# Contiguous groups of four from the ninth period on, in an attention kernel that shares its exponentials between two engines

## The chip, the cores and the metric

The kernel runs on one core of a Trainium2 chip. Its engines are TensorE (PE, matrix products), VectorE (DVE), ScalarE (ACT), GpSimd (POOL) and SyncE (SP, which issues transfers); they run side by side and meet at semaphores. The metric is the device time of one execution in microseconds (us), the median over several runs. Beside it there is one profiled execution, whose trace gives the duration of every instruction.

## The reference

Two attention blocks with the same input are mixed by a gate, position by position:

```python
x = A_x                                        # 1 x 2048 x 512, bf16
g = sigmoid((x * gate_w).sum(-1, keepdims=True))
a = _A_ref(x, A_wqkv, A_wo)                    # full attention, 32 heads of 16
b = _B_ref(x, B_wqkv, B_wo)                    # each position looks at 8 keys: itself and 2, 4 ... 14 back
return g * a + (1 - g) * b
```

Part A is a full softmax attention over 2048 x 2048 scores for each of 32 heads. Part B takes for every position a softmax over only eight keys, two positions apart.

## The kernel before, in words

**Part A.** The work is cut into 32 periods: four chunks of 512 queries times eight groups of four heads. A period has 64 blocks, one for each of 16 tiles of 128 keys and each of four heads; a block is 128 keys x 512 queries. The last period is done in two halves of 256 queries, so the program has 33 entries in its tables. For most blocks PE makes the scores in a PSUM tile `ring`, ACT takes their exponential into `pT` (three blocks in one instruction and two in the next, in turn), and PE multiplies `pT` with the values `vp_all` and adds up in one accumulator bank of the period. At the end of a period DVE transposes the accumulator out of PSUM (`accT`), takes a reciprocal (`rden`), POOL scales (`rden`, `ott`), and DVE transposes the result into `oat`, which the output projection reads.

**Blocks on DVE.** `n_dve` says how many blocks of each period go past ACT. They are taken from the last four key tiles and are worked on in groups (`d_set`): three blocks a group (`NGR`) in periods below `FLAT0`, four (`NGF`) from there on. For each block PE makes the scores in a spare PSUM bank, and DVE turns them into the bits of a bf16 power of two with one multiply-add to integers (`p1`, 512 elements, written to the group's buffer `dt`). When a group is full, three integer additions (`sh`, `NV` - 1 of them) make three shifted copies of the whole group in `pd_a`, and PE multiplies the four versions with differently weighted values (`vp_all`, `vd_all`); their sum approximates the exponential. In a group of three, a pass reads the 1536 elements as six rows of 256 and writes rows that lie 514 elements apart; in a group of four, a pass reads and writes one run of 2048 elements.

The group buffers `dt` lie in `dt_a` for early periods, then in `dt_a` and in `wkv` (the weights of the key and value projections, 4096 elements a partition, which are no longer needed by then). For groups of four they lie in `bw`, the weights of part B, free only when the last projection of part B is done.

**Part B.** Sixteen tiles of 128 positions. SP loads shifted keys and values (`ksh`, `vsh`), POOL forms products and sums (`prod`, `lg`, `av`, `obb`), DVE and ACT do the small softmax (`mx`, `ssum`, `rr`, and `lg`), POOL issues some additions as transfers (`av<-prod`, `av<-av`; the last two tiles add on POOL instead). PE transposes `obb`, DVE copies it to `obt`, and the output projection adds it to part A. `b_start` and `b_space` give the planned time of each tile.

**The order.** Nothing is ordered at run time. Every step is recorded with an engine, a due time and a cost; `list_schedule` plays them through by its own cost figures (`SB`, `PT`, `TT`, `GP` and others, where a part marked `True` occupies a port that DVE and POOL share in the plan) and the resulting order is written into the program. Each engine executes its list strictly in that order and waits where an operand is not there.

Of the kernel before, what the change touches and what calls it, by code (L numbers as in the profile page):

```python
# [12 lines left out]
BF16 = mybir.dt.bfloat16  # L13
# [3 lines left out]

CFG = dict(
    set_sizes=(3, 2),
    n_dve=(3, 3, 6, 6, 9, 9, 12, 12) + (12,) * 19 + (16,) * 4 + (8, 4),  # L20
    dve_tiles=4,
    b_start=36.0,
    b_space=(43.0,) * 16,
    chain=("pe", "dve", "act", "pool", "sp"),
)

# [1 line left out]
DH = 16  # L28
NG = 8
W = 8  # L30
DIL = 2
QW = 512
NEG = -1.0e9
FLAT0 = 27
BITS = 128.0
LN2 = 0.6931471805599453
SHIFT = 175.0
# [1 line left out]
NV = 4  # L39
NGR = 3  # L40
NGF = 4
NK1 = 2
# [7 lines left out]
NDE = 1  # L50
NDL = 3
# [57 lines left out]
PVU, PVN = 100.0, 4  # L109
GP = lambda kind, n: [(False, PRE), (True, NS[kind] * n)]  # L110
SB = lambda n: [(True, 0.065 + n / 3840.0)]
PT = lambda n: [(True, 0.1 + n / 3840.0)]
TT = lambda n: [(True, 0.075 + n / 960.0)]
PASS, SWITCH, KEEP, RIDE, ALONE = 0.22, 0.1, 1.2, 50.0, 3.0
WAIT, FREE, LATE, CLAMP = 0.15, 0.1, 10.0, -1.0
# [192 lines left out]
def kernel(  # L308
# [19 lines left out]
    DC = D // 128  # L328
# [6 lines left out]
    const = ctx.enter_context(tc.tile_pool(name="const", bufs=1))  # L335
# [90 lines left out]
    n_dve = cfg["n_dve"]  # L426
# [4 lines left out]
    for pi in range(NP):  # L431
        first_unit.append(nu)
        n = n_dve[pi]
        gr = group_of(pi)
# [16 lines left out]
    for pi, (own, groups) in enumerate(seq):  # L451
        n = sum(len(g) for g in groups)
# [22 lines left out]

    wkv = const.tile([128, DC, 2 * D], BF16, name="wkv")
    wq = const.tile([128, DC, D], BF16, name="wq")
    wq2 = const.tile([128, DC, 8, 2, DH], BF16, name="wq2")
    q_scr = tc.dram_tile([NG * NC // 2 * 16, DH * QW], BF16, name="q_scr")
    wk3 = const.tile([128, DC, NK1, 2, DH], BF16, name="wk3")  # L480
    a_w3 = A_wqkv.rearrange("(c p) n -> p c n", p=128)
    wkp = const.tile([128, DC, (NG - NK1) // 2, 4, 2, DH], BF16, name="wkp")
    gw = const.tile([128, DC], BF16, name="gw")
    bw = const.tile([128, DC, 3 * D], BF16, name="bw")
    bwo = const.tile([128, DC, D], BF16, name="bwo")
# [22 lines left out]
    wkv_l = wkv[:].rearrange("p c n -> p (c n)")  # L508
    dt_bufs = [dt_a[:, k_ * NGR * QW:(k_ + 1) * NGR * QW] for k_ in range(NDE)]
# [319 lines left out]
    for h0, h1, pn in ((4, 8, 1), (8, 16, 2), (16, 24, 4), (24, 32, 6)):  # L829
        TB = 512 // ((h1 - h0) * DH)  # L830
        for tb in range(0, NT, TB):
            late = tb + TB > NT - NTD
# [3 lines left out]
    qt_tiles, o_q, q_tok, last_q = {}, {}, {}, [None]  # L836
# [120 lines left out]
    a = None  # L957
    for sc in range(NC):
        a = op("pe", 0.9, zmm(sc), GT + sc, full=1, deps=[o_bw, a] + o_xt[sc], alloc=[tzp] if sc == 0 else [],
               use=[tzp] if sc else [], rel=20.0)  # L960
    a = op("act", 0.25, zsig, GT + 5, deps=[a], use=[tzp])
    o_g = op("dve", 0.8, zgate, GT + 6, deps=[a])
    a = op("pe", 1.2, zrows, GT + 8, full=1, deps=[o_g, o_init_p], alloc=[tzr])
    o_gr = op("dve", 0.12, zcopy, GT + 9, deps=[a], use=[tzr])


    o_kvd, o_obt, bw_users = [], [], []
    obt_tiles, obt_tok = {}, {}
    WP = WH // 2
    HB = D // 2  # L970
# [1 line left out]
    def b_tile(t):  # L972
# [27 lines left out]
        a = op("pe", WAVE(2), proj("pk", 1, 0), tb - 34 - KB, full=2, deps=[o_bw] + o_xt[cb], alloc=[tk, tkv], rel=rel)  # L1000
        a = op("pe", WAVE(2), proj("pk", 1, 2), tb - 33.5 - KB, full=2, deps=[a], use=[tk])
        ka = op("dve", 0.61, ke, tb - 33 - KB, deps=[a], use=[tk, tkv])
        tk = tok("misc", 2)
        a = op("pe", WAVE(2), proj("pv", 2, 0), tb - 32 - KB, full=2, deps=[o_bw] + o_xt[cb], alloc=[tk], rel=rel, after=[a])
        a = op("pe", WAVE(2), proj("pv", 2, 2), tb - 31.5 - KB, full=2, deps=[a], use=[tk])
# [4 lines left out]

        def qe():
            V.tensor_scalar(out=st["qb"][:], in0=st["pq"][:], scalar1=float(DH) ** -0.5, scalar2=None, op0=ALU.mult)
        bw_users.append(a)
        tk = tok("misc", 2)
        a = op("pe", WAVE(2), proj("pq", 0, 0), tb - 24 - QB, full=2, deps=[o_bw] + o_xt[cb], alloc=[tk, tqb], rel=rel)
        a = op("pe", WAVE(2), proj("pq", 0, 2), tb - 23.5 - QB, full=2, deps=[a], use=[tk])
        bw_users.append(a)
        qa = op("dve", 0.61, qe, tb - 23 - QB, deps=[a], use=[tk, tqb])

        def load(key, off, hf):  # L1020
# [154 lines left out]
        for g_ in range(len(halves)):  # L1175
# [5 lines left out]
        a = op("dve", 0.34, sm_pre, tb + SMD, deps=[l1], use=[tlg])  # L1181
        a = op("dve", 0.0, sm_sub, tb + SMD, deps=[a], use=[tlg], parts=TT(H * W)) if SM_V else op(
            "pool", 0.0, sm_sub, GFIRST, deps=[a], use=[tlg], parts=GP("ff", H * W))
# [126 lines left out]
                pv_run(pend[q_:min(n, q_ + 4)], tn)  # L1310
            del pend[:n]

    bw_l = bw[:].rearrange("p c n -> p (c n)")
    wkv_users = [o for o in ops if o.eng == "pe" and o.name.startswith(("kp", "vp"))]
    d_st, d_last, d_sh = {}, [None, None], []
    d_count, d_ends = [0, 0, 0, 0], []

    def d_set(pi, gi, t, j, qk_, tn):

        c_, i = periods[pi]  # L1320
        late = pi >= LATE0
        flat, gr = pi >= FLAT0, group_of(pi)
        key = (pi, gi)
        first = key not in d_st
        if first:
            slot = d_count[3] % NDL if flat else d_count[0] % NDL if late else d_count[2] % NDE
            d_count[3] += flat
            d_count[0] += late and not flat
            d_count[2] += not late
            d_st[key] = dict(dt=bw_l[:, slot * gr * QW:(slot + 1) * gr * QW] if flat else dt_bufs[slot],  # L1330
                             td=tok("dtf", NDL) if flat else tok("dtl", NDL) if late else tok("dt", NDE), js=[], ts=[], p1=[])
        g = d_st[key]
        n_ = len(g["js"])
        g["js"].append(j)
        g["ts"].append(t)

        st = {}
        tx = tok("misc", 2)

        def dq():  # L1340
            st["x"] = misc_ps([128, QW])
            for t_, cs in parts_of(pi, t):
                mm(st["x"][:, cs], kt_all[32 * j:32 * j + 32, i, t_ * 128:(t_ + 1) * 128], qt_tiles[pi][32 * j:32 * j + 32, q_cols(pi)],
                   True, True, tile_position=(32 * j, 0))

        def p1():
            V.tensor_scalar(out=g["dt"][:, n_ * QW:(n_ + 1) * QW].bitcast(U16), in0=st["x"][:], scalar1=float(DH) ** -0.5 * BITS / LN2,
                            scalar2=(127.0 + DEXP + SHIFT * float(DH) ** -0.5 / LN2) * BITS, op0=ALU.mult, op1=ALU.add)
        deps = [o_q[pi], o_k[i][tiles_of(pi, t)[0] // TPC]] + [o_vd[(4 * i + j, t_)] for t_ in tiles_of(pi, t)]
        if first and flat and d_count[3] <= NDL:  # L1350
            deps += bw_users
        elif first and late and d_count[0] <= NDL:
            deps += wkv_users + d_ends[-NV * NDE:]
        a = op("pe", 0.0, dq, tn - 3.0, mode="r", js=[j], deps=deps, alloc=[tx] + ([g["td"]] if first else []),
               use=[q_tok[pi]] + ([] if first else [g["td"]]), after=[qk_, d_last[1]], ride=True, name=f"dq{pi}")
        d_last[1] = a
        o = op("dve", 0.61, p1, tn + P1D, deps=[a], use=[tx, g["td"]], after=[d_last[0]], name=f"p1_{pi}")
        d_last[0] = o
        g["p1"].append(o)
        if len(g["js"]) < gr:  # L1360
            return
        vs = [o_vd[(4 * i + j_, t2)] for t_, j_ in zip(g["ts"], g["js"]) for t2 in tiles_of(pi, t_)]

        def sh(m, pb):
            def s():
                o_, i_ = pb.bitcast(U16)[:, :, 0:QW], g["dt"].bitcast(U16)
                if not flat:
                    i_ = _ap(i_, [list(i_.ap[0]), [QW // 2, 2 * NGR], [1, QW // 2]])
                else:
                    o_ = o_.rearrange("p q n -> p (q n)")  # L1370
                V.tensor_scalar(out=o_, in0=i_, scalar1=STEP * m, scalar2=None, op0=ALU.add)
            return s

        def pv(m, pb):
            def s():
                pv_mm(pi, [(t_, j_, pb[:, n1, 0:QW]) for n1, (t_, j_) in enumerate(zip(g["ts"], g["js"]))],
                      lambda t2: vd_all[:, m - 1, t2 - (NT - NTD)] if m else vp_all[:, t2])
            return s

        def dpv(m, pb, deps, use, dl):  # L1380
            b = op("pe", 0.0, pv(m, pb), dl, mode="c", js=g["js"], full=1, deps=deps + [o_t0[pi]] + vs,
                   use=[use, acc_tok[pi]], name=f"dpv{pi}")
            o_pv[pi].append(b)
            d_ends.append(b)
        dpv(0, g["dt"].rearrange("p (q n) -> p q n", q=gr), list(g["p1"]), g["td"], tn + 4.5)
        for m in range(1, NV):
            pb = pd_bufs[d_count[1] % NPD]
            if flat:
                k0 = d_count[1] % NPD * gr * QW
                pb = pd_a[:, k0:k0 + gr * QW].rearrange("p (q n) -> p q n", q=gr)  # L1390
            d_count[1] += 1
            tp = tok("pd", NPD)
            a = op("dve", 0.0, sh(m, pb), tn + 1.5 + SHD * (m - 1), deps=list(g["p1"]), alloc=[tp], use=[g["td"]],
                   lat=(0.065 + NGR * QW / 1920.0 if not flat else 0.1 + gr * QW / 3840.0) + SH_LAT, after=d_sh[-1:],
                   parts=[(False, 0.065 + NGR * QW / 1920.0)] if not flat else PT(gr * QW), name=f"sh{pi}")
            d_sh.append(a)
            dpv(m, pb, [a], tp, tn + 4.5 + SHD * m)
# [216 lines left out]
```

## Time and profile before

| | before |
|---|---|
| time, median of 3 runs | 800.21 us (799.62 to 801.82) |
| the profiled execution: time / span of its instructions | 803.18 / 800.3 us |
| busy PE / DVE / ACT / POOL, share of the span | 93% / 87% / 97% / 81% |
| exponentials on ACT, `pT<-ring` | 674 instructions, 766.5 us |
| integer passes `pd_a` in groups of three | 288 (138 from `dt_a`, 150 from `wkv`), mean 0.94 us |
| integer passes `pd_a` in groups of four, from `bw` | 57, mean 0.744 us |
| granted TensorE clock, mean | 0.998 |

The span runs from the first to the last instruction; the time of the execution has 2.9 us more. Busy shares are the union of an engine's instructions, and two that follow each other closely overlap by some hundredths of a microsecond in the records, so a mean duration is a little more than what one instruction costs in a row. The first group of four is worked on from 684 us on.

### The profile page before, as it was taken

The numbers are of one execution on the slowest core, as the hardware profiler recorded it, in microseconds if no ns is written. First come the engines' busy times: TensorE is split into PE (matmuls) and PEld (weight loads), VectorE is DVE, ScalarE is ACT, GpSimd is POOL, SyncE is SP. The second block draws the span as 40 slices with busy tenths as digits, with TensorE's granted clock in tenths as the row PEclk, the third lists the DMA queues.
The fourth block names the chain that finished last, engine by engine and source line by source line (L and its number), as shares of the span: only waits on it lengthen the run. The fifth ranks groups of instructions, "written<-read, shape, count | busy, mean of one in ns | idle before, by whom it ended". The sixth has DMA issues, their size and how long they took to land.

```text
span 800.3 us, 17773 instructions
## 1 busy us (share of the span) xinstructions
PE 741.5 (93%) x6817; PEld 241.9 (30%) x6876; DVE 692.6 (87%) x1100; ACT 774.5 (97%) x697; POOL 644.3 (81%) x1067
## 2 busy tenths in 40 slices
PE   8999989999999999999999999998999999999997
PEld 4333333233222222222222232232232232222233
DVE  5638787998887899999998899899898999988986
ACT  3999999999999999999999999999999999999996
POOL 4098989899999997899989899999989999991000
PEclk9999999999999999999999999999999999999999
DMA  8413071625344535336352626253625371100000
GB/s 265 115 46 106 21 177 47 156 64 128 98 113 118 131 83 143 81 97 142 73 146 77 162 74 165 66 117 112 144 65 109 107 169 35 47 8 20 2 2 28
DMA packets 58886, 77.21 MB, mean 96 GB/s; under 512 B 3744, under 2 KB 50848, under 8 KB 58800
## 3 DMA queue, kind: packets, MB, share of 16 engines
q1 hardware_dynamic: 52608, 53.91, 21.6%
q0 software_dynamic: 6048, 22.02, 14.8%
q8 instruction: 53, 0.87, 0.4%
q14 instruction: 33, 0.27, 0.1%
q10 hardware_dynamic: 144, 0.13, 0.0%
HBM read 43.78 MB, written 10.26 MB: 68 GB/s over the span
## 4 chain that ended last, share of the span: by engine, by line
ACT 50%; PE 23%; issue 22%; DVE 4%; DMA 1%; SPq 0%; ACTq 0%; DVEq 0%
ACT pT L370 49%; PE misc_ps L379 15%; PE ring L379 7%; DVE pd_a L370 1%; DMA xld<-in_A_x_dram 1%; DVE dt_a L370 1%; ACT lg L370 1%; DVE vd_all L370 1%; DVE wkv L370 0%; DVE kt_all L370 0%; PE pxt L647 0%; DVE vp_all L370 0%; DVE ssum L370 0%; DVE rr L370 0%; DVE osb L370 0%
## 5 line engine op out<-in xcount | busy, mean ns | idle before, releaser
L370 ACT ACTIVATE pT<-ring 128x1536 bf16<-128x1536 f32 (+1 forms) x674 | 766.5, 1327 | 10.5 <-PE ring L379 7.3
L379 PE MATMUL ring<-qt,kt_all 32*128 32x512 bf16 (+1 forms) x1736 | 265.5, 375 | 41.3 <-ACT pT L370 32.8
L379 PE MATMUL misc_ps<-pT,vp_all 128*17 128x512 bf16 (+3 forms) x1736 | 201.9, 377 | 0.3 <-DVE dt_a L370 0.2
L370 POOL TENSOR_TENSOR prod<-ksh,qb 128x256 f32<-128x256 bf16 x256 | 175.7, 757 | 30.0 <-DMA ksh<-kv_scr 27.2
L379 PEld LDWEIGHTS <-kt_all 32*128 32x128 bf16 x2112 | 92.2, 91 | 291.2 <-issue 281.6
L370 POOL TENSOR_TENSOR prod<-prod 128x256 f32<-128x256 f32 (+1 forms) x256 | 172.8, 690 | 5.9
L370 DVE TENSOR_SCALAR pd_a<-wkv 128x1536 uint16<-128x1536 uint16 x150 | 137.2, 940 | 1.0 <-PE misc_ps L379 0.6
L379 PE MATMUL misc_ps<-qt,kt_all 32*128 32x512 bf16 (+1 forms) x376 | 130.5, 374 | 3.8 <-DVE dt_a L370 2.2
L379 PE MATMUL misc_ps<-pd_a,vd_all 128*17 128x512 bf16 (+1 forms) x1128 | 131.1, 375 | 0.5 <-DVE pd_a L370 0.4
L379 PE MATMUL misc_ps<-z 128*32 128x512 bf16 x382 | 127.9, 388 | 1.6 <-DVE z L370 1.6
L370 DVE TENSOR_SCALAR pd_a<-dt_a 128x1536 uint16<-128x1536 uint16 x138 | 126.5, 939 | 0.6
L370 DVE TENSOR_SCALAR wkv<-misc_ps 128x512 uint16<-128x512 f32 x150 | 100.1, 681 | 18.5 <-PE misc_ps L379 17.6
L370 DVE TENSOR_SCALAR dt_a<-misc_ps 128x512 uint16<-128x512 f32 x138 | 92.1, 682 | 21.0 <-PE misc_ps L379 19.6
L370 POOL TENSOR_TENSOR prod<-vsh,lg 128x256 f32<-128x256 bf16 x128 | 84.1, 772 | 0.0
L379 PEld LDWEIGHTS <-vp_all 128*17 128x17 bf16 (+1 forms) x2112 | 55.9, 88 | 84.8 <-issue 71.9
L370 POOL TENSOR_TENSOR av<-vsh,lg 128x256 f32<-128x256 bf16 x128 | 80.0, 664 | 0.0
L370 DVE TENSOR_SCALAR bw<-misc_ps 128x512 uint16<-128x512 f32 x76 | 50.8, 684 | 10.8 <-PE misc_ps L379 10.2
L379 PE MATMUL misc_ps<-bw,xT 128*128 128x512 bf16 x163 | 50.6, 384 | 1.9 <-issue 1.4
L379 PEld LDWEIGHTS <-vd_all 128*17 128x17 bf16 x1128 | 34.9, 88 | 53.4 <-issue 46.6
L379 PEld LDWEIGHTS <-z 128*32 128x32 bf16 x382 | 32.9, 96 | 45.5 <-issue 26.5
L370 DVE TENSOR_SCALAR pd_a<-bw 128x2048 uint16<-128x2048 uint16 x57 | 41.2, 744 | 0.1
L370 POOL TENSOR_TENSOR rden<-rden,g_rw 128x16 f32<-128x16 f32 x30 | 9.3, 310 | 37.5 <-DVE rden L370 37.4
(100 smaller groups left out, 596.0 us busy)
## 6 DMA issues: line engine op xcount, KB each, us to landing
ksh<-kv_scr SPq DMA_DIRECT2D x32, 512.0 KB
vsh<-kv_scr SPq DMA_DIRECT2D x32, 512.0 KB
av<-prod POOLq DMA_DIRECT2D x28, 512.0 KB, 6.2
av<-av POOLq DMA_DIRECT2D x14, 512.0 KB, 5.0
kv_scr<-kvs SPq DMA_DIRECT2D x16, 256.0 KB
qt<-q_scr SPq DMA_DIRECT2D x30, 128.0 KB
out_dram<-osb SPq DMA_DIRECT2D x15, 128.0 KB
xld<-in_A_x_dram SPq DMA_DIRECT2D x3, 512.0 KB
```

The costliest lines, as they stand in the source:

```text
L370: return chain_on(key, f(*a, **k))
L379: return chain(nc.tensor.matmul(out, lhsT=lhsT, rhs=rhs, start=start, stop=stop, **kw))
```

## The change

Groups of four begin with period 8 instead of period 27. In periods 8 to 26, `n_dve` alternates between 12 and 16 where it was 12, so that 400 blocks go to DVE instead of 364. The spacing of the last twelve tiles of part B in the plan is 46 us instead of 43. In the plan, a contiguous pass costs 0.5 us off the shared port and 0.25 us on it, where it was 0.633 us on it. The buffers of groups of four are now two in `wkv` and one in a new tile `wx`, which holds what were the tiles `wq2` and `wkp` (weights for the projections of the early periods); the first three groups wait until these weights have been used. The instructions of POOL are the same 1073 as before.

```diff
 CFG = dict(
-    n_dve=(3, 3, 6, 6, 9, 9, 12, 12) + (12,) * 19 + (16,) * 4 + (8, 4),
+    n_dve=(3, 3, 6, 6, 9, 9, 12, 12) + (12, 16) * 9 + (12,) + (16,) * 4 + (8, 4),
-    b_space=(43.0,) * 16,
+    b_space=(43.0,) * 4 + (46.0,) * 12,
...
-FLAT0 = 27
+FLAT0 = 8
...
-PT = lambda n: [(True, 0.1 + n / 3840.0)]
+PT = lambda n: [(False, 0.5), (True, 0.25)]
...
-    wq2 = const.tile([128, DC, 8, 2, DH], BF16, name="wq2")
+    n_q2, n_kp = DC * 8 * 2 * DH, DC * (NG - NK1) // 2 * 8 * DH
+    wx = const.tile([128, n_q2 + n_kp], BF16, name="wx")
+    wq2 = wx[:, 0:n_q2].rearrange("p (c h e d) -> p c h e d", c=DC, h=8, e=2)
+    wkp = wx[:, n_q2:n_q2 + n_kp].rearrange("p (c i j e d) -> p c i j e d", c=DC, i=(NG - NK1) // 2, j=4, e=2)
...
-    bw_l = bw[:].rearrange("p c n -> p (c n)")
+    dt_flat = [wkv_l[:, 0:NGF * QW], wkv_l[:, NGF * QW:2 * NGF * QW], wx[:, 0:NGF * QW]]
...
-            d_st[key] = dict(dt=bw_l[:, slot * gr * QW:(slot + 1) * gr * QW] if flat else dt_bufs[slot],
+            d_st[key] = dict(dt=dt_flat[slot] if flat else dt_bufs[slot],
...
-        if first and flat and d_count[3] <= NDL:
-            deps += bw_users
-        elif first and late and d_count[0] <= NDL:
-            deps += wkv_users + d_ends[-NV * NDE:]
+        if first and late and d_count[3 if flat else 0] <= NDL:
+            deps += wkv_users + [o_q[1]] + d_ends[-NV * NDE:]
```

More of the change, by code (lines that the diff above doesn't have):

```diff
@@ L481 @@
     a_w3 = A_wqkv.rearrange("(c p) n -> p c n", p=128)
-    wkp = const.tile([128, DC, (NG - NK1) // 2, 4, 2, DH], BF16, name="wkp")
     gw = const.tile([128, DC], BF16, name="gw")
@@ L964 @@
     o_gr = op("dve", 0.12, zcopy, GT + 9, deps=[a], use=[tzr])
-    o_kvd, o_obt, bw_users = [], [], []
+    o_kvd, o_obt = [], []
     obt_tiles, obt_tok = {}, {}
@@ L1012, in qe @@
             V.tensor_scalar(out=st["qb"][:], in0=st["pq"][:], scalar1=float(DH) ** -0.5, scalar2=None, op0=ALU.mult)
-        bw_users.append(a)
         tk = tok("misc", 2)
@@ L1016, in b_tile @@
         a = op("pe", WAVE(2), proj("pq", 0, 2), tb - 23.5 - QB, full=2, deps=[a], use=[tk])
-        bw_users.append(a)
         qa = op("dve", 0.61, qe, tb - 23 - QB, deps=[a], use=[tk, tqb])
```

## The prediction

> **What bounds the kernel now.** First the page's busy shares, then its chain of waits, then the slices.
>
> ```profile
> PE 741.5 (93%) x6817; PEld 241.9 (30%) x6876; DVE 692.6 (87%) x1100; ACT 774.5 (97%) x697; POOL 644.3 (81%) x1067
> ACT  3999999999999999999999999999999999999996
> POOL 4098989899999997899989899999989999991000
> ACT 50%; PE 23%; issue 22%; DVE 4%; DMA 1%; SPq 0%; ACTq 0%; DVEq 0%
> ```
>
> ACT is the bound: 97% busy, and half of the chain. POOL is the second thing to see: it is full from slice 2 to slice 36 and then has nothing left. Its 81% is an average of "full" and "done". The last instruction of part B on POOL is an `obb` pair at 721.56 us, 1.41 us long, so POOL ends its tiles at 723.0, 77 us ahead of the end. That is all the slack it has.
>
> The groups by form give the prices on ACT and DVE; the same view cut to two stretches shows the contiguous pass beside a working POOL (684 to 722) and beside an idle one (722 to 801):
>
> ```profile
> L370 ACT ACTIVATE pT<-ring 128x1536 bf16<-128x1536 f32 x337 | 518.3, 1538 | 9.8 <-PE ring L379 7.3 <-PE misc_ps L379 1.9
> L370 ACT ACTIVATE pT<-ring 128x1024 bf16<-128x1024 f32 x336 | 375.5, 1117 | 0.7 <-PE misc_ps L379 0.3
> L370 DVE TENSOR_SCALAR pd_a<-wkv 128x1536 uint16<-128x1536 uint16 x150 | 137.2, 940 | 1.0 <-PE misc_ps L379 0.6
> ...
> L370 DVE TENSOR_SCALAR pd_a<-bw 128x2048 uint16<-128x2048 uint16 x16 | 14.3, 908 | 0.1
> ...
> L370 DVE TENSOR_SCALAR pd_a<-bw 128x2048 uint16<-128x2048 uint16 x41 | 27.0, 680 | 0.1
> ```
>
> The same instruction takes 0.68 us alone and 0.91 beside POOL. The timelines of the two engines around 700 us show the other half of it:
>
> ```profile
> 698.60 0.68 DVE L370 TENSOR_SCALAR pd_a<-bw 128x2048 uint16<-128x2048 uint16 x1
> 699.80 3.23 DVE L370 TENSOR_SCALAR pd_a<-bw 128x2048 uint16<-128x2048 uint16 x3
> 703.54 1.13 DVE L370 TENSOR_SCALAR pd_a<-bw 128x2048 uint16<-128x2048 uint16 x1
> ...
> 698.04 7.13 POOL L370 TENSOR_TENSOR av<-vsh,lg 128x256 f32<-128x256 bf16 x8
> 705.13 2.88 POOL L370 TENSOR_TENSOR prod<-vsh,lg 128x256 f32<-128x256 bf16 x4
> 712.28 2.44 POOL L370 TENSOR_TENSOR prod<-vsh,lg 128x256 f32<-128x256 bf16 x4
> 714.68 1.86 POOL L370 TENSOR_TENSOR av<-av,prod 128x256 f32<-128x256 f32 x2
> ```
>
> From 712.28 to 714.68 POOL makes four products with no pass beside them: 0.60 us each. From 698.04 to 705.13 it makes eight such, with five passes beside them, and needs 7.09 us instead of 4.80: **each contiguous pass costs POOL 0.46 us**. Over all of 684 to 722, POOL's groups exceed their undisturbed durations (the medians of 0.65 for the two products, 0.72 for f32 adds) by 8 x 0.28 + 11 x 0.11 + 12 x 0.08 + 8 x 0.24 = 6.3 us, and two small steps by 0.35 (`rden`, 0.57 instead of 0.22) and 0.2 (`rr`): 6.9 us for 16 passes, 0.43 each. I take 0.45. The passes of groups of three show no such thing: with some 160 of them in 300 to 640, `av<-vsh` keeps its mean of 0.65.
>
> **ACT.** 36 blocks less: 766.5 us for 1684 blocks is 0.455 a block, so **-16.4 us**. If ACT stays the bound, that is the gain in full.
>
> **DVE.** In the built program 228 passes of 1536 go (288 to 60) and 198 of 2048 come (57 to 255). A pass of three costs 0.88 in a row (1.80 us for two, 2.65 for three in the timeline): -200 us. The new passes take 0.60 in a row beside an idle POOL and 1.05 in the worst row (3.23 for three); taken at 0.908 less an overlap of 0.08, +164. 36 more `p1` at 0.60: +22. Sum -14 us, bounds -59 and +30. DVE was busy 422.9 us of the 459 between 225 and 684, so at the middle value it keeps pace, no better.
>
> **PE.** A group of four has its four heads in four column groups, so its products run side by side; in periods 8 to 26 there are 66 groups x 4 sets of products instead of 76 x 4. 36 more score products ride with the others. Filler products on zeros go from 380 to 334. Nothing here is near the end.
>
> **Buffers.** The first group of four now waits for `wkv` and `wx` to be free. The last products that read `wkv` are at 182 us and period 8 starts at about 225: no cost; if they came late, three groups would wait at most.
>
> **POOL.** It has the same instructions, and 255 - 16 = 239 more passes to suffer. At 0.45 all colliding cost 107.6 us; POOL was idle 35.7 of the 497 us from 225 to 722, so some 7% of the passes may fall into a gap: **+100 us**. What can be recovered are waits for DVE, since a late POOL finds these results ready:
>
> ```profile
> POOL av L370 <- DMA av<-prod: 7.8, 4, 3.1
> POOL av L370 <- POOL prod L370: 5.7, 19, 0.3
> POOL rden L370 <- DVE rden L370: 4.9, 9, 1.5
> POOL lg L370 <- DVE mx L370: 3.1, 5, 0.8
> POOL prod L370 <- DVE qb L370: 2.0, 1, 2.0
> POOL rr L370 <- DVE rr L370: 1.7, 3, 0.8
> ```
>
> The last four sum to 11.7; POOL's own chains and its transfers remain. So POOL ends at 723 + 100 - 12 = **811 us**. Bounds: with no gap found and nothing recovered 831; with 0.40 a pass, one pass in ten free and all 35.7 us of idle time gone, 773, where ACT would decide.
>
> One page of the Trainium skill speaks against this change. "SBUF — State Buffer", section "Who interferes with whom", says that a DVE operation in a two-port mode and GpSimd exclude each other for the whole instruction. By that rule the price would be the full record, 0.68 us, and POOL would end some 50 us later still; the 0.46 of the row decides, as the records of neighbouring instructions overlap. The same page ("SBUF: two separate sides") says that transfers issued by GpSimd starve too, as it cannot write their descriptors. No trace here shows it, because the last such issue is at 644 us, ahead of the first pass; by it no issue would be a gap, and the 7% would go, for some 7 us more.
>
> **The order decides that POOL's delay counts.** In DVE's built list the last `obt` copy, part B's last tile, stands third from the end behind all 255 passes; before, it stood behind 26 of 57 contiguous passes with two more periods to come. PE's last real work is the transpose of that `obb`, the projection of `obt`, and one product of `oat`. So the plan already puts the end of POOL right ahead of the end of the program, and it charges a pass 0.25 us on the shared port where the trace shows 0.45. And DVE runs its list in order: `mx` waits for POOL's `lg`, `oat` for POOL's `ott`. When POOL is late, DVE stands at these with the `p1` and evictions queued behind; then PE has no free bank and ACT no scores. ACT can't run ahead and simply finish early.
>
> **The tail** behind POOL's last `obb`: four transposes 0.4, `obt` 0.41, seven projections 1.7 (0.82 for three at 794.02), eviction 0.69, last product 0.38, and from the final add (796.79) to the span's end 3.5; with five handovers of some 0.2, 8 us. The span becomes 811 + 8 = 819. The profiled execution has 2.9 us around its span and lies 3.0 above the median, so the median is the span: **819 us**, 19 slower.
>
> **Rivals.**
> 1. *ACT keeps the bound (faster).* POOL's slack of 77 us swallows the locks and the end is 800.2 - 16.4 = **784 us**. For: ACT is the bound today, and POOL had slack. Against: POOL would have to end by 784 - 8 = 776, that is, 239 passes may cost (776 - 711)/239 = 0.27 us each. The trace has 0.43 to 0.46. It decides if four passes in ten miss POOL.
> 2. *DVE becomes the bound.* POOL pays less than the row says but DVE pays its full 0.91 waiting: 422.9 - 200 + 180 + 22 = 425 us of work, at the 92% that it reached 461 us long, where ACT needs 443: 784 + 18 = **802 us**. It decides above 0.82 a pass, just under what I took; against it, the wait of DVE and the delay of POOL come from the same collisions.
> 3. *The passes lose their fast form* in `wkv` and `wx`: 1.25 us each (4/3 of 0.94), DVE +63 and some **850 us**. Against: type, size and layout are those of the row from `bw`.
>
> **Chances.** POOL bound 0.74, ACT bound 0.16, DVE bound 0.08, slow form 0.02. POOL's own range is 800 to 838, from 0.40 a pass with half the idle time recovered to everything colliding. The whole range reaches into rival 1, to 790, leaving out about 0.13 below and 0.05 above. A difference under 0.3% (797.8 to 802.6) can't be told from none. Faster: rival 1 and a little of the main case, 0.18. Same: half of rival 2 and the low end of the main case, 0.06. Slower: 0.76.
>
> **What would show it.** POOL's digits at 9 up to the last slices and its last `obb` within 10 us of the end; `av<-vsh` and `prod` groups longer by 0.2 to 0.3 in the mean; `pd_a` from `wkv` and `wx` at 0.9; DVE waiting for POOL in `mx` and `oat`; ACT with 40 us or more of idle time. It is wrong if POOL is done by 775, or if its groups keep their means beside the passes.

## The result and the profile after

The changed kernel takes **851.2 us** (848.5 to 854.0) against 800.7 for the kernel before in the same runs: a ratio of 1.063, 95% interval 1.059 to 1.067. The forecast had the right sign and the wrong size: 819, with 838 as the upper end. The profiled execution has 851.43 us and a span of 849.4.

The page's busy shares, slices and chain:

```profile
PE 755.9 (89%) x6885; PEld 232.9 (27%) x6939; DVE 736.2 (87%) x1106; ACT 765.1 (90%) x682; POOL 731.1 (86%) x1067
ACT  3999999999999798998999969989798989979993
POOL 4198999998999886899899979989798988969996
DVE 33%; PE 28%; ACT 24%; issue 14%; DMA 1%; SPq 0%; ACTq 0%; DVEq 0%
```

POOL now works to the end; its last `obb` ends at 841.9 us. But no engine is full. ACT has lost its 97%, POOL has 86%, and the chain, half of it ACT before, now runs through DVE for a third. This is what engines that wait for each other in turn look like. The groups by form, and the waits from 225 us on, say where:

```profile
L370 DVE TENSOR_SCALAR pd_a<-wkv 128x2048 uint16<-128x2048 uint16 x171 | 180.5, 1077 | 0.5
L370 DVE TENSOR_SCALAR pd_a<-wx 128x2048 uint16<-128x2048 uint16 x84 | 90.0, 1091 | 0.2
...
PE misc_ps L379 <- DVE pd_a L370: 37.4, 46, 3.0
ACT pT L370 <- PE ring L379: 32.3, 33, 4.1
ACT pT L370 <- PE misc_ps L379: 22.1, 20, 4.1
POOL rden L370 <- DVE rden L370: 20.0, 10, 4.2
POOL rr L370 <- DVE rr L370: 18.7, 7, 7.6
```

A contiguous pass takes 1.08 us in the mean, not the 0.908 of the stretch from 684 to 722 before. PE waits for passes (up to 3.0 us at once), ACT for PE (up to 4.1), and POOL for DVE's small steps: 38.7 us in the last two lines, where it was 6.6 before. The timelines of DVE, POOL and ACT in one such place:

```profile
485.50 3.70 DVE L370 TENSOR_SCALAR pd_a<-wkv 128x2048 uint16<-128x2048 uint16 x1
489.13 0.68 DVE L370 TENSOR_SCALAR wx<-misc_ps 128x512 uint16<-128x512 f32 x1
489.73 4.55 DVE L370 TENSOR_SCALAR pd_a<-wkv 128x2048 uint16<-128x2048 uint16 x1
...
484.74 0.88 POOL L370 DMA_DIRECT2D av<-prod  x1 [0.30 <-POOL prod L370]
485.34 0.94 POOL L370 TENSOR_TENSOR lg<-lg,mx 128x256 f32<-128x256 f32 x1
485.94 2.71 POOL L370 TENSOR_TENSOR prod<-vsh,lg 128x256 f32<-128x256 bf16 x4
488.94 0.88 POOL L370 DMA_DIRECT2D av<-prod  x1 [0.30 <-POOL prod L370]
489.55 2.83 POOL L370 TENSOR_TENSOR prod<-ksh,qb 128x256 f32<-128x256 bf16 x4
492.07 1.66 POOL L370 TENSOR_TENSOR prod<-prod 128x256 f32<-128x256 f32 x2
497.95 0.54 POOL L370 TENSOR_TENSOR rden<-rden,g_rw 128x16 f32<-128x16 f32 x1 [4.23 <-DVE rden L370]
...
490.51 1.02 ACT L370 ACTIVATE pT<-ring 128x1024 bf16<-128x1024 f32 x1 [2.73 <-PE ring L379]
495.59 1.45 ACT L370 ACTIVATE pT<-ring 128x1536 bf16<-128x1536 f32 x1 [4.06 <-PE ring L379]
```

Two passes, of a kind that takes 0.6 us alone, take 3.7 and 4.55. Beside the first, POOL runs five steps in a row; beside the second, six. Both times POOL has just issued a transfer (484.74, 488.94), and both times the pass ends half a microsecond after POOL's run of steps. ACT stands still for 2.7 and 4.1 us, and then POOL itself waits 4.2 us for DVE's `rden`. The forecast's prices, 0.45 us on POOL and 0.908 on DVE, were those of a milder exchange: in the stretch that they come from, the longest pass took 1.13 us. In the trace of the changed kernel 21 passes are longer than 1.3 us. They lie 38.1 us in all above 1.13, and all passes together 41.0. All 21 begin within 4 us behind an issue of POOL (42 passes begin there); of the other 213 none is so long.

### The profile page after: what moved, and what is told of

It reads as the page before. It is cut to its first block, busy times and chain, and to the rows that moved or that the text cites. A ratio compares the mean times of both kernels' runs of the same rounds, so it can differ in the third digit from the quotient of the medians.

```text
span 849.4 us, 17863 instructions
## 1 busy us (share of the span) xinstructions
PE 755.9 (89%) x6885; PEld 232.9 (27%) x6939; DVE 736.2 (87%) x1106; ACT 765.1 (90%) x682; POOL 731.1 (86%) x1067
## 4 chain that ended last, share of the span: by engine, by line
DVE 33%; PE 28%; ACT 24%; issue 14%; DMA 1%; SPq 0%; ACTq 0%; DVEq 0%
ACT pT L370 24%; PE misc_ps L379 20%; DVE pd_a L370 17%; PE ring L379 8%; DVE wkv L370 6%; DVE wx L370 4%; DVE kvs L370 1%; DMA xld<-in_A_x_dram 1%; DVE osb L370 1%; DVE dt_a L370 1%; DVE vd_all L370 1%; DVE accT L370 0%; DVE oat L370 0%; DVE kt_all L370 0%; PE pxt L649 0%
## 5 line engine op out<-in xcount | busy, mean ns | idle before, releaser
L370 POOL TENSOR_TENSOR prod<-ksh,qb 128x256 f32<-128x256 bf16 x256 | 194.4, 814 | 33.6 <-DMA ksh<-kv_scr 32.7
L370 POOL TENSOR_TENSOR prod<-prod 128x256 f32<-128x256 f32 (+1 forms) x256 | 197.9, 786 | 5.3
L370 DVE TENSOR_SCALAR pd_a<-wkv 128x2048 uint16<-128x2048 uint16 x171 | 180.5, 1077 | 0.5
L370 DVE TENSOR_SCALAR wkv<-misc_ps 128x512 uint16<-128x512 f32 x228 | 151.1, 679 | 24.2 <-PE misc_ps L379 21.8
L379 PE MATMUL misc_ps<-pd_a,vd_all 128*17 128x512 bf16 (+1 forms) x1236 | 122.6, 384 | 38.1 <-DVE pd_a L370 37.4
L379 PE MATMUL misc_ps<-z 128*32 128x512 bf16 (+1 forms) x337 | 115.5, 401 | 3.2 <-DVE z L370 1.6
L370 DVE TENSOR_SCALAR pd_a<-wx 128x2048 uint16<-128x2048 uint16 x84 | 90.0, 1091 | 0.2
L370 DVE TENSOR_SCALAR wx<-misc_ps 128x512 uint16<-128x512 f32 x112 | 73.8, 679 | 14.9 <-PE misc_ps L379 14.1
L370 DVE TENSOR_SCALAR pd_a<-dt_a 128x1536 uint16<-128x1536 uint16 x60 | 54.6, 942 | 0.4
L370 DVE TENSOR_SCALAR dt_a<-misc_ps 128x512 uint16<-128x512 f32 x60 | 39.8, 684 | 13.8 <-PE misc_ps L379 13.0
L379 PEld LDWEIGHTS <-xT 128*128 128x128 bf16 x576 | 29.0, 98 | 35.9 <-issue 33.7
```

Source lines behind the costliest of these rows:

```text
L370: return chain_on(key, f(*a, **k))
L379: return chain(nc.tensor.matmul(out, lhsT=lhsT, rhs=rhs, start=start, stop=stop, **kw))
```

## The experiments

Theory A: contiguous passes and POOL exclude each other, at a cost to both; A1 adds that POOL keeps DVE off for several steps in a row behind a transfer that it issued. Rivals: the load (B: 400 blocks are too many for DVE and PE), the order (C: the low price or the wider spacing). Where a run gives a sum "above 1.13", it is that of all its contiguous passes. The code cuts show the main lines of each edit only.

### POOL's steps made short

All POOL steps of part B on 16 columns, for instance:

```diff
-                G.tensor_tensor(out=st["prod", hf, wp][:, w_, c0:c0 + HB], ...
+                G.tensor_tensor(out=st["prod", hf, wp][:, w_, c0:c0 + DH], ...
...
```

> The changed kernel with the same order on DVE, PE and ACT, but each step of part B on POOL works on 16 columns instead of 256 and its transfers are replaced by such short adds (part B is left out of the output that way), so POOL hardly touches the memory beside the contiguous passes. Theory A (passes and POOL exclude each other, and this costs both): passes fall to a mean of 0.68 us, none over 0.8, and the time falls to what ACT needs, 782 to 795 us. Theory B (400 blocks, the planned order and its prices overload DVE and PE, POOL has little to do with it): over 835 us.

Measured: 789.2 us, 0.986 of the kernel before (0.983 to 0.989), span 787.0.

```profile
PE 734.1 (93%) x6939; PEld 233.6 (30%) x6939; DVE 646.6 (82%) x1106; ACT 758.0 (96%) x682; POOL 302.0 (38%) x1069
L370 DVE TENSOR_SCALAR pd_a<-wkv 128x2048 uint16<-128x2048 uint16 x171 | 119.6, 719 | 1.9 <-PE misc_ps L379 1.3
```

With the same order on DVE, PE and ACT, and the same 400 blocks, ACT is the bound again at 96%. So all that the change loses, it loses beside POOL. Rival B falls: the load and the order fit once POOL is out of the way. The passes are at 0.72 in the mean. Three take 1.4 to 2.1 us, where none over 0.8 was expected. They stand beside POOL's `obb` steps, which kept their size, and POOL issues no transfer in this kernel. So an issue is not the only place where a pass can wait this long; what happens there was not followed up.

### POOL's transfers replaced by adds

```diff
-                    G.dma_start(out=av[:, wp:wp + WP, :], in_=st["av", wp][:], accum_op=ALU.add)
...
+                G.tensor_tensor(out=av[:, d_, 0:HB], in0=av[:, d_, 0:HB], in1=a_, op=ALU.add)
```

> The changed kernel with the same order, but each of the 42 transfers that POOL issues (av<-prod, av<-av) is replaced by one POOL add of 256 columns, about as long as the issue (0.7 against 0.9 us); the rest of these sums is left out. Theory A1 (the passes of 1.4 to 4.6 us, 21 of them and 41 us above 1.13, come from what POOL does right after issuing a transfer): no pass over 1.3 us, POOL still longer by 0.45 per pass, time 808 to 825 us. Theory A2 (the long passes come from any run of POOL steps): some 20 long passes stay, time 843 to 855 us.

Measured: 808.8 us, 1.010 (1.007 to 1.014), span 807.4.

```profile
PE 747.4 (93%) x6939; PEld 232.8 (29%) x6939; DVE 697.6 (86%) x1106; ACT 762.3 (94%) x682; POOL 737.8 (91%) x1067
L370 DVE TENSOR_SCALAR pd_a<-wkv 128x2048 uint16<-128x2048 uint16 x171 | 157.5, 942 | 0.9 <-PE misc_ps L379 0.5
```

POOL has as much to do as in the changed kernel (737.8 against 731.1 us), DVE has the same list, and the span is 42 us shorter. No pass is over 1.3 us. POOL's last `obb` ends at 798: this kernel ends as the forecast said, behind a full POOL, even some 10 us earlier. Two lesser things went with the transfers: POOL's waits for their landing (3.9 us in the changed kernel from 225 us on), and a part of the loss of PE's granted clock (0.988 here, 0.966 there).

### The same transfers issued by SP

```diff
...
-                    G.dma_start(out=av[:, wp:wp + WP, :], in_=st["av", wp][:], accum_op=ALU.add)
+                    SP.dma_start(out=av[:, wp:wp + WP, :], in_=st["av", wp][:])
```

> The changed kernel with the same order on DVE, PE and ACT, but the 42 transfers of part B (av<-prod, av<-av) are issued by SP's queue, as plain copies of the same bytes without adding (the sums are left out that way); POOL issues none. If the issue by POOL is what starves DVE (theory A1): no pass over 1.3 us, POOL has 37 us less to do, 790 to 810 us. If the moving data does it: 15 or more passes of over 1.3 us stay and the time is over 830 us.

Measured: 802.2 us, 1.002 (1.000 to 1.003). The profiled execution has 806.3 us and a span of 804.1.

```profile
PE 747.2 (93%) x6939; PEld 231.5 (29%) x6939; DVE 701.5 (87%) x1106; ACT 762.3 (95%) x682; POOL 705.4 (88%) x1025
L370 DVE TENSOR_SCALAR pd_a<-wkv 128x2048 uint16<-128x2048 uint16 x171 | 158.5, 948 | 0.5
```

No pass is over 1.3 us; the mean of all 255 is 0.953. The same bytes still move into the same memory at the same places of the program. So the data in flight alone doesn't make the long passes; the issue by POOL does, or something that comes with it. The edit also takes the addition out of the transfer, and adding and issuing by POOL were not separated. POOL's last `obb` ends at 797.

### A wait behind each issue

```diff
+                V.memset(meet[:, n_meet[0]:n_meet[0] + 1], 0.0)
+                G.tensor_copy(out=met[:], in_=meet[:, n_meet[0]:n_meet[0] + 1])
...
```

> The changed kernel, complete, with one addition: right behind each of the 42 transfers that POOL issues, POOL copies one element a partition that DVE has written at that place of its own order, so POOL waits for DVE once and its next steps don't start ahead of time. If steps that POOL starts early behind an issue are what keeps DVE off the memory (theory A1): at most 5 passes over 1.3 us instead of 21, their 41 us mostly gone, 812 to 832 us, since each meeting costs POOL up to half a microsecond. If the wait changes nothing about who gets the memory: 15 or more long passes and 850 us or more.

Measured: 831.1 us, 1.035 (1.025 to 1.044); 16 long passes instead of 21, 23 us instead of 41 above 1.13. The time is inside the expectation, the count is not. The view of the waits shows why:

```profile
POOL met L370 <- DVE meet L370: 4.4, 4, 2.2
```

In 38 of 42 places POOL did not stand idle for DVE's mark. The records that tell of early starts (0.85 us or more, with the next step 0.70 us or less behind) are as many as in the changed kernel, 86 against 80. So the edit was no clean test. It supports the part that long passes play, 18 us off their sum and 20 off the time, but it doesn't show what ends such a run of POOL.

### Rows at a pitch

```diff
...
-                    k0 = d_count[1] % NPD * gr * QW
-                    pb = pd_a[:, k0:k0 + gr * QW].rearrange("p (q n) -> p q n", q=gr)
+                    k0 = d_count[1] % NPD * gr * ROW
+                    pb = pd_a[:, k0:k0 + gr * ROW].rearrange("p (q n) -> p q n", q=gr)
```

> The changed kernel with the same order, groups of four and 400 blocks, but each pass writes rows of 512 that lie 514 elements apart and reads eight rows of 256, as the groups of three do, so that it is not contiguous. Theory A: a pass takes 1.2 us whatever POOL does, POOL's groups return to the durations of before (av<-vsh 0.65, busy 645 us, its last obb 30 us or more ahead of the 840 us of the changed kernel), and DVE decides with 255 x 1.17 = 298 us of passes against 270 now: 805 to 830 us. Theory B: the load on DVE is larger than now, so 855 us or more.

Measured: 852.6 us, 1.065 (1.054 to 1.076). The experiment failed in its aim, and teaches something else:

```profile
L370 DVE TENSOR_SCALAR pd_a<-wkv 128x2048 uint16<-128x2048 uint16 x171 | 178.5, 1065 | 0.5
```

The passes are as fast and as disturbed as contiguous ones: 73 of the 255 take less than 0.70 us (72 in the changed kernel), and 22 take more than 1.3 (21 there). Being contiguous is not what makes them so. What differs from the groups of three, 0.94 us for 1536 elements and at most 0.96, is the count of rows: six read and three written there, eight and four here. This agrees with the Trainium skill, "VectorE: DVE Perf Modes", section "What auto-detection actually checks": the mode that uses both ports asks for outer dimensions of source and destination that are both even, or equal. Other pairs of counts were not tried.

### Fewer blocks

```diff
-    n_dve=... + (12, 16) * 9 + (12,) + (16,) * 4 + (8, 4),
+    n_dve=... + (12,) * 19 + (16,) * 4 + (8, 4),
```

> The changed kernel with 12 blocks in each of the periods 8 to 26 (364 blocks, 228 contiguous passes instead of 255), all else as changed; the planner makes a new order. Theory A: 27 collisions less, some 12 us less on POOL and 27 us less on DVE, while ACT has 16 us more: 825 to 843 us, still far above the kernel before. Theory B: with the number of blocks of before the time falls to 800 to 812 us.

Measured: 853.1 us, 1.066 (1.062 to 1.069). Rival B is out here too: the number of blocks of before doesn't bring the time back. But theory A missed as well, by 10 us. There are 20 long passes with 37.6 us above 1.13. With a ninth of the passes gone, 19 would have been expected if their number went with the passes and 21 if it went with the transfers, so this run can't tell the two apart. It shows something else: POOL's last `obb` ends at 818.5 us, 32 us ahead of the end, and ACT's last exponential at 842.1. ACT has 15 us more work here, but it is also idle for long: a POOL that is done early doesn't free ACT from its waits (45.1 us between exponentials from 225 us on, 54.4 in the changed kernel).

### More blocks in groups of three

```diff
 # in the kernel before
-    n_dve=... + (12,) * 19 + ...
+    n_dve=... + (12, 15) * 9 + (12,) + ...
```

> The kernel before with another part of the change alone: more blocks on DVE in every second of the periods 8 to 26, but in groups of three (15 instead of 12, 27 blocks more), so that no pass there collides with POOL. ACT has 12 us less to do, DVE 27 x 1.48 = 40 us more, on an engine that is 92% busy from 225 to 684 us. If DVE is what limits more blocks: 815 to 845 us. If POOL alone is the matter: 788 to 800 us.

Measured: 871.5 us, 1.089 (1.070 to 1.108), worse than expected. POOL is undisturbed, 646 us busy. More blocks without the fast form don't fit on DVE; the gain on ACT needs the fast form, and the fast form collides.

### The plan's parts

The changed kernel with the old price:

> The changed kernel planned with the old price of a contiguous pass (0.633 us on the shared port instead of 0.5 off it and 0.25 on it); the planner makes another order, the instructions are the same. If collisions decide (theory A), an order that knows of them can't remove them: 835 to 860 us. If the order made with the low price is the cause (theory C): below 820 us.

Measured: 870.9 us, 1.088 (1.082 to 1.095), 11 above the expected range. 18 long passes, 34 us above 1.13; and the last exponential ends at 829 us, the last `obb` at 859, so part B alone fills the end. The low price isn't the culprit; the one order made with the higher price is worse.

The kernel before with the spacing of the change:

> The kernel before with one part of the change alone: the last twelve tiles of part B planned 46 us apart instead of 43. POOL then ends some 36 us later, at about 759 us, still 40 ahead of the end. Theory A: no effect, 798 to 803 us. If late tiles of part B hold up the rest by themselves (theory C): 806 us or more.

Measured: 806.8 us, 1.007 (1.005 to 1.009): 6 us that I expected to be none, and within what had been set for theory C (806 or more). So the wider spacing costs something by itself, about an eighth of the 50 us of the change; the forecast had no term for it. `pd_a` from `bw` rises from 0.744 to 0.810 in the mean, as part B now meets more of the late passes; whether that is the whole of the 6 us was not separated.

### Contiguous groups behind, or nearly behind, the last transfer

```diff
...
-FLAT0 = 8
+FLAT0 = 26      # the other: 23
...
```

Both also take the old spacing of 43 us and other block counts, as their expectations say, and the wait of the first groups for their buffers is set to the number of contiguous buffers.

> The changed kernel with the contiguous groups from period 26 on instead of 8, so that they begin behind the last transfer that POOL issues, 16 blocks in period 26 and 12 in each of 8 to 25 (368 blocks, 69 contiguous passes), and the old spacing of 43 us. Theory A: no pass over 1.3 us; ACT has 4 blocks less than the kernel before, 1.8 us, and POOL 12 more collisions, 5 us of its 77 us of slack: 797 to 801 us. If contiguous passes or the buffers in wkv and wx cost something by themselves: 806 us or more.

Measured: 806.7 us, 1.006 (1.003 to 1.009).

> As the one from period 26, but from period 23 on, with 12 and 16 blocks in turn in 23 to 26 (372 blocks, 99 contiguous passes): ahead of the last six transfers or so. Theory A: 42 more collisions than the kernel before, 19 us on POOL, within its slack; 2 to 4 passes over 1.3 us beside the transfers, 3 to 8 us; ACT has 3.6 us less: 799 to 806 us. If long passes came with any crowded stretch, more than 8 of them and over 810 us.

Measured: 815.3 us, 1.015 (1.009 to 1.021). The long passes are as forecast, none from period 26 and 2 from period 23; the times are 6 and 9 us above the ranges. The 806.7 is even within what was set for a cost of the passes or the buffers by themselves (806 or more). The executions say a little more. From period 26 the time goes with PE's granted clock, from 803.5 us at 0.995 to 809.5 at 0.987, and the kernel before beside it does the same: 803.8 at 0.996, 808.1 at 0.987. At a like clock the two are within 3 us of each other, so a good part of the difference goes with the clock, and what lowers the clock is open. From period 23 some 5 us are left at a like clock (812.9 at 0.986), which these runs don't resolve. None of the kernels that compute everything beats the one before.

## Why the prediction was wrong

**Right: the mechanism, POOL's price and the tail.** POOL and the contiguous passes exclude each other, and ACT's saving disappears. The tail behind the last `obb` was put at 8 us: 849.4 - 841.9 = 7.5. The price on POOL was nearly right: where it can be seen by itself, in the run with SP's transfers, POOL is 705.4 us busy and has lost 37 us of issues, so 239 more passes cost 705.4 + 37 - 644.3 = 98 us, 0.41 each (forecast: 100).

**Wrong: "what can be recovered are waits for DVE, since a late POOL finds these results ready".** From 225 us to its last `obb`, POOL was to have 561.3 us of work (461.3 before, plus 100) and 23.7 us idle (35.7 less 12), ending at 811 in round numbers. It had 551.3 and 65.6. The work came out 10 below, the idle time 42 above: 811 - 10 + 42 = 843 (841.9 measured). The recovered 12 us should have been 30 lost: the last two lines of waits in the section on the result grew from 6.6 to 38.7 us. POOL was not the one late engine that everyone waits for; it waited for DVE in turn. Without long passes the step holds: in the run with adds in place of the transfers, the same two waits sum to 3.0 us.

**Wrong: the price of a pass on DVE, "taken at 0.908".** It was 1.08, and the difference isn't spread evenly. Of 255 passes, 234 behave as the stretch from 684 to 722 said (0.914 in the mean), and 21 take 1.4 to 4.6 us. That stretch held no issue of POOL: the last one was at 651.1 us (the forecast said 644), and its mean was taken for passes that would lie beside 33 of them. Without collisions the time is 789.2 us. With collisions but no issue by POOL it is 802.2 (with SP's transfers, where POOL has 37 us less to do) or 808.8 (with adds, where it has as much to do): 13 to 20 us. POOL's issues make it 851.2, another 42 to 49.

**Wrong: the path, "When POOL is late, DVE stands at these".** DVE was to wait at `mx` and `oat` for a late POOL. In the trace of the changed kernel none of DVE's waits above 0.15 us ends with POOL. DVE was held inside its passes, and that reached ACT directly: from 225 us on, PE waited 37.4 us for passes (0.4 before) and ACT 54.4 us for PE (2.0 before). ACT's exponentials, before and after, in the pages' lines:

```profile
L370 ACT ACTIVATE pT<-ring 128x1536 bf16<-128x1536 f32 (+1 forms) x674 | 766.5, 1327 | 10.5 <-PE ring L379 7.3
L370 ACT ACTIVATE pT<-ring 128x1536 bf16<-128x1536 f32 (+1 forms) x659 | 756.5, 1281 | 62.9 <-PE ring L379 37.9
```

The work fell by 10 us and the idle time before it rose by 52, so the last exponential ends at 836.3 instead of 793.4, just 5.6 us ahead of POOL's last `obb`. Both engines were late together. POOL's end was where the forecast had it, but it decided the last few microseconds only: with POOL done earlier, ACT's last exponential would still have come 43 us later than before. The run with fewer blocks is such a case.

**The signs named ahead.** POOL's late `obb` and ACT's idle time came. The groups `av<-vsh` and `prod` were to be longer by 0.2 to 0.3 us in the mean; on the pages they are longer by 0.02 to 0.12. That sign didn't fit the forecast's own sum either: 100 us over the 768 instructions of these groups are 0.13 each.

**A row that was there.** The trace of before has other DVE instructions that take much longer near an issue of POOL. The view of the tile `qa`:

```profile
L370 DVE TENSOR_SCALAR qa<-qs x15: 282/413/1404, 22.9 to 729.6; 128x256 uint32<-128x256 uint32 x15
```

The three figures are the least, the median and the longest in nanoseconds. The same instruction takes 0.28 us at best. The two longest, 0.97 us at 490 and 1.40 at 570, began 0.9 and 1.1 us behind a transfer's issue; of the other 13 none began so close behind one. A pass over 2048 elements of `kt_all` took 1.81 us, where the shortest took 0.72, and began 0.4 us behind an issue. A mean and a median hide this; the maximum beside them asks the question.

**Transfers that starve.** The forecast put 7 us on issues that stop being gaps. POOL's issues themselves grew by just 0.04 us in the mean (0.88 to 0.92), and the medians from issue to landing stayed where they were (6.2 us, and 5.0 against 5.1). The harm was the other way round: the steps behind an issue held DVE, at 42 us or more. The Trainium skill, "SBUF — State Buffer", section "Who interferes with whom", also says that whoever issues first gets the pair for the whole instruction and that issue order decides who blocks. The trace agrees that a pass can wait for POOL; here a long pass stood beside two to six of POOL's instructions, and not beside one.

**The rivals.** ACT keeping the bound would have needed passes that POOL doesn't feel; with POOL's steps short it gives 789, close to the 784 of that rival. DVE as the bound names the right engine for a third of the chain, but by waiting, not by load: with POOL's steps short it is 82% busy. The 850 us of the third rival lie next to the 851.2 measured, by chance: the passes kept their fast form, as 72 of the 255 take less than 0.70 us and the shortest 0.63.

## What to carry to other kernels

When two engines exclude each other, the cost isn't a price per collision alone: look for the place where one of them runs several instructions ahead, and read the maximum of the shared form's duration in every stretch, beside every kind of neighbour. Two engines with in-order lists that wait for each other turn one long instruction into idle time on all of them, so "a late engine finds its inputs ready" holds only if the other one isn't late for the same reason. And before a form of instruction is spread from one stretch to the whole program, ask what else is absent from the stretch that its price was taken from.

## What the runs showed of the hardware

- Behind the issue of a transfer, POOL's next steps appear in the records with mostly 0.8 to 1.0 us where such steps take 0.65 to 0.72 undisturbed, still some 0.6 us apart: they start 0.2 to 0.35 us ahead of the end of their predecessors. Of the 728 products and adds of 256 columns, 80 in the changed kernel and 112 in the kernel before have such a record (0.85 us or more, the next step 0.70 us or less behind), all within 6 us behind an issue by POOL; in the two runs in which SP issues the transfers or adds take their place there are none.
- In these runs of steps a contiguous pass on DVE stood beside two to six of them; with the same bytes moved by SP, no pass was over 1.3 us. That the early start is what shuts DVE out is an inference: the wait put behind each issue left most early starts in place, and 16 of the long passes.
- A pass over 2048 elements of 16 bits took 0.63 us at best with rows at a pitch of 514 as well as contiguous. With three rows written and six read, over 1536 elements, it never took less than 0.89.
- PE's granted clock was 0.966 in the mean (0.998 before) and lowest, 0.73, in the stretch from 275 to 300 us, where ACT was busy 19.5 of 25 us; with POOL's steps short it was 0.998 again. What part of the lost time comes from the lower clock was not separated.
